# Top-k attention and expert layer on one core: weight pieces through a queue, and the first three batches routed sooner

## The chip, the core and the metric

The kernel runs on one core of a Trainium2 chip. A core has TensorE (PE: matmuls, with the weight loads PEld beside them), VectorE (DVE), ScalarE (ACT), GpSimd (POOL) and SyncE (SP, which here issues most DMAs). They run side by side and wait for each other by semaphores. The metric is the device time of one execution in microseconds (us), as the median of several runs; lower is better.

## What is computed

Attention over 8 batches of 8 heads, 576 rows of 64 numbers, where each row of scores keeps its 32 largest; then an expert layer, in which each of the 4608 rows of 512 numbers goes to the one of 8 experts that its logits choose:

```python
scores = scale * np.matmul(q, k.transpose(0, 1, 3, 2))
kth = np.partition(scores, -top_k, axis=-1)[..., -top_k:-top_k + 1]
scores = np.where(scores >= kth, scores, -1000000000.0)
attn = np.exp(scores - np.max(scores, axis=-1, keepdims=True))
attn = attn / (np.sum(attn, axis=-1, keepdims=True) + 1e-09)
x = np.matmul(attn, v)          # then (B, H, S, D) -> (B * S, H * D)

logits = x @ w_gate + modality_bias[modality_id]
e_idx = np.argmax(logits, axis=1)
gate_w = probs[np.arange(N), e_idx]      # probs: softmax of the logits
for e in range(E):
    mask = e_idx == e
    h = np.maximum(x[mask] @ w1[e], 0.0)
    out[mask] = gate_w[mask, None] * (h @ w2[e])
```

## The kernel before

The attention is cut into 288 tiles of 128 rows by 576 scores; nine tiles make the two heads of a pair, four pairs a batch, so a batch is 36 steps. One loop (`for i in range(LAST)`, L1105) runs over all tiles, one per step, as a pipeline: step `i` makes the scores of tile `i + 2` on PE (`scores`, L1113), lets ACT copy them to `Ssb` (`sevac`, L385), and on DVE takes the largest of six pieces of tile `i` (`subs`, L391) and merges those of tile `i - 1` (`chain`, L396). The sign of the scores against the 24th largest (ACT, `sign`, L421) times the scores (POOL, `pool_y`, L429, tile `y`) gives DVE the next eight (`find`, L434). The 32nd is then known, and the exponentials below it are dropped. For two in three of the first 48 tiles this goes by `hide` on DVE, `hidden` on POOL (tile `ex`, L469) and `masked` on ACT; for all others by `expo` on ACT and `keep` on DVE (tile `P`, L456), and POOL reads one element of `P` as a gate (L479). Nine steps later PE transposes the probabilities (`trans`), ACT copies them, and PE multiplies them by v (`av`, L518). `j = i % 9` is the place in a pair.

For the pairs ahead, q and k are loaded on SP's queue at `j` 5 and 6, v at 7; PE transposes them (`prep`) at `j` 0 (the tail), 1 (k) and 3 (q), and DMAs on the same SP queue stack their halves one step later (`moves`: tiles `ks` at L332, `qs` at L334). The scores need both.

Once a batch is through, it is routed in steps counted by `r`: logits (L563) at r 0, their transposes (L572) and DVE's products `lt` (L580) at r 1, the rows of x (L551, L552) at r 2 to 4, then `route`: a one-hot `ohb` of the best expert, ACT's exponential `r_ez`, rank matmuls against triangular matrices (`ranks`, L597) and ACT's copy `r_rk`, the sum `r_sm`, and the places `dest`. Five indirect DMAs of POOL (`send`, L609) scatter the rows into a buffer `xs` sorted by expert. The small DVE steps stand in the list `side`, of which each step takes up to 12, to the next `PAUSE`; `rush` goes ahead of it.

As soon as rows enough are there (`more_moe`, L873), a slot of 256 rows of one expert is picked, gathered (`rows`, L699, tile `xg`) and computed in small pieces, which each step takes as long as a budget in microseconds, `spare_pe`, allows: transposes of the rows, `hid` (w1, L790) and `outp` (w2, L802). The weights of a slot are eight DMAs of 512 KB on SP's queue, four pieces of `w1b` (L722) and four of `w2b` (L726); each goes out when the slot before has used its piece (`used`, L736), or from the lists of `more_moe`. Slots 0 to 13 are computed beside the attention, slots 14 to 18 after it at higher precision (`slot`, L1043). Where PE has no expert work, `keep_warm` (L950) gives it matmuls of constants whose results nobody reads.

Of the kernel before, what the change touches and what calls it, by code (L numbers as in the profile page):

```python
# [13 lines left out]
AF = mybir.ActivationFunctionType  # L14
# [15 lines left out]
NW = 3  # L30
# [14 lines left out]
TL = LR + 2  # L45
# [12 lines left out]
PJ0 = (1, 2, 3)  # L58
FAST = 7
RXQ = (2, 3, 3, 4, 4)  # L60
SNQ, RNQ = 12, 18
# [14 lines left out]
def kernel(  # L76
# [13 lines left out]
    V, A, G, PE, SP = nc.vector, nc.scalar, nc.gpsimd, nc.tensor, nc.sync  # L90
    B, H, S, D = q.shape
# [493 lines left out]

    def route(lg, bias, oh, x5b, wait=0):

# [19 lines left out]
        def send(c):  # L607
# [14 lines left out]
                                    op=OP.is_equal),  # L622
            PAUSE,
            *[PAUSE] * wait,
            lambda: A.activation(ez, z, AF.Exp),
            ranks,
            PAUSE,
# [27 lines left out]
    def sched(s, whole):  # L655

        o = {"w1": {}}
        SL[s] = o  # L660
# [63 lines left out]

    def load_w2(s, g):
        SP.dma_start(w2b[:, 2 * g:2 * g + 2, :],  # L726
                     w2[ds(SL[s]["e"], 1), g * 256:g * 256 + 256, :].rearrange("o (c p) d -> p (o c) d", p=128))

    def expert(s, act, nxt, whole, defer):
# [6 lines left out]
        def used(x, load):  # L736

            o["used"][x] += 1
            if o["nxt"]:
                chore.append(lambda g=o["used"][x] - 1: load(s + 1, g))  # L740
                if not defer:
                    chores()
# [31 lines left out]
        def xt_next(c):  # L774
# [7 lines left out]
            SL[s + 1]["early"] = c == 2  # L782

        def hid(f, c0):
            if f % 2 == 0 and c0 == 0:
                room()
                o["ps"] = tile_e([128, 2, SLOT], f // 2)
            ps = o["ps"]
            for c in range(c0, c0 + HG):
                PE.matmul(ps[:, f % 2], w1b[:, c, f * 128:(f + 1) * 128], xgT[:, c, :],  # L790
                          start=(c == 0), stop=(c == KC - 1))
            if f % 2 == 0 or c0 + HG < KC:
                return
            post(lambda: A.activation(hT[:, f - 1:f + 1, :], ps, AF.Relu) if act else  # L794
                 V.tensor_scalar(hT[:, f - 1:f + 1, :], ps, 0.0, None, op0=OP.max))
            used(0, load_w1)

        def outp(f, t):
            if f == 0:
                room()  # L800
                o["py"] = tile_e([128, Dm], t)
            PE.matmul(o["py"], hT[:, f, t * 128:(t + 1) * 128], w2b[:, f, :], start=(f == 0), stop=(f == FC - 1))  # L802
            if f % 2 == 1 and t == 1:
                used(1, load_w2)
            if f == FC - 1:
                post(lambda py=o["py"]: result(t, py))
# [63 lines left out]
    plan = {"ready": -1, "go": False}  # L870
    alone = [False]

    def more_moe():  # L873
# [14 lines left out]
        elif full >= n + 1:  # L888
# [11 lines left out]
            def take(x, g):  # L900
                return lambda: (load_w1, load_w2)[x](n, g) if g < free[x] else None
            l1 = [take(0, g) for g in range(4)]
            l2 = [f for g in range(4) for f in (take(1, g), PAUSE)]
            go = [lambda: plan.update(go=True)]
            if n == 0:
                def sent():

                    while sends:
                        sends.popleft()()
                rush.extend(pick + [begin] + l1[:2] + done + [PAUSE, sent] + rows + go + [PAUSE, l1[2], l1[3], PAUSE] + tok)  # L910
            else:
                begun, rest = ([], go) if moe else (go, [])
                rush.extend(pick + [begin] + rows + rest + l1[:1] + done + [PAUSE, l1[1], l1[2], PAUSE, l1[3]] + begun + [PAUSE] + tok)
# [71 lines left out]
    for x in range(QL):  # L985
# [5 lines left out]
        sevac(x)  # L991
    keep_warm(NW)
    ok = lambda x: 0 <= x < NT
# [111 lines left out]
    for i in range(LAST):  # L1105
# [48 lines left out]
        cost += COST["rest"] * (len(lp) > 0)  # L1154
        part = (PREP if p else PREP0).get(j)
        if p + 1 < NPAIR and part:
            prep(p + 1, part)
            cost += COST["t" if part == "t" else "prep"]
        if p + 2 < NPAIR and j in LJ:
            load(p + 2, "kq"[LJ.index(j)])  # L1160
        if j == VJ and p < NPAIR:
            load(p, "v")
        b1, r = divmod(i - (TL + 2), 36)
        b1 -= 1
        if 0 <= b1 < B:
            if r == 0:
# [13 lines left out]
            if r == rl[1] + (1 if early_route(b1) else 2):  # L1180
                steps, store = route(lgb[b1 % 2], bias_all[:, b1], ohb[b1 % 2], x5, int(FAST <= b1 < B - 1))
                side.extend(steps)

                def done(n=b1 + 1):
                    seen[0] = n * S
                    fresh.clear()
                if b1 == 0:
                    side.extend([store.pop(), done])
            if r == max(rl[1], rx[4]) + (1 if early_route(b1) else 2):
                if b1 == 0:  # L1190
# [10 lines left out]
        if ok(u) and role(u) in (3, 7, 8):  # L1201
            f = av(u // 9, role(u), xTs(u // 36)[(u // 9) % HP])
            if role(u) == 7:
                avs.extend(f)
            else:
                f[0][1]()
                avs.extend(f[1:])
                cost += f[0][0]
# [63 lines left out]
        arrange(ops, *end)  # L1272

        for f in moves:
            f()
# [19 lines left out]
        if ok(i - 2) and (i - 2) % 3 == 2:  # L1295
            small(i - 4)
        if i == CLOSE:
            alone[0] = True
            S0 = nslot[0]
# [159 lines left out]
```

## Time and profile before

| | us |
|---|---|
| median of 3 runs | 1208.47 (1208.12 to 1208.58) |
| the profiled execution | 1207.26 |
| its span, first to last instruction | 1205.5 |
| PE busy in the span | 1158.7 |
| DVE busy | 1100.4 |
| ACT busy | 982.4 |
| POOL busy | 677.0 |

The profile is one execution, whose every instruction has a start and a duration. A view by line groups equal instructions; the timeline shows them in order with the idle time ahead of one and what ended it; the waits sum this idle time; the busy time by stretch shows when an engine was full, and the granted clock of TensorE as a share of 2.4 GHz (1.00, or 0.50 for 1.2 GHz). An engine's idle time costs only where others wait for it.

### The profile page before, as it was taken

Reading aid. Unit: us, or ns where it says so; the run is one execution under the profiler, and the core shown is the slowest. Engines: PE = TensorE matmul, PEld = TensorE weight load, DVE = VectorE, ACT = ScalarE, POOL = GpSimd, SP = SyncE. Lnnn points to the kernel's source line nnn. Section 1 sums busy time; section 2 is a strip of 40 time slices with the busy share of each in tenths; the row PEclk is TensorE's granted clock in tenths of the full one; section 3 lists DMA queues with packets and bytes.
Section 4 is the critical chain, followed back from the end, with each engine's and each line's share of the span. In section 5 each row is a group of like instructions: output and inputs, shape, how many; then the busy total and the mean of one; then the engine's idle time right before and its main releaser. Section 6 shows DMA issues by size and latency. Waiting matters only on the chain.

```text
span 1205.5 us, 28005 instructions
## 1 busy us (share of the span) xinstructions
PE 1158.7 (96%) x7914; PEld 908.5 (75%) x7914; DVE 1100.4 (91%) x5474; ACT 982.4 (81%) x2015; POOL 677.0 (56%) x1256
## 2 busy tenths in 40 slices
PE   8889979999999999999899999999999999999998
PEld 6766767778687877778587776878687777589987
DVE  7999999999999999999999999999998999376772
ACT  6999979998798988998799888989898888355652
POOL 6888875564755566556556566557655655121011
PEclk9899999999999999999999999999999999999999
DMA  5563358663585638664865657665665653287750
GB/s 127 157 180 88 88 157 228 170 166 88 158 235 146 166 103 256 159 168 122 215 184 145 173 148 192 171 158 148 169 194 146 177 156 123 82 274 248 254 196 22
DMA packets 204323, 197.09 MB, mean 163 GB/s; under 512 B 104413, under 2 KB 151533, under 8 KB 204160
## 3 DMA queue, kind: packets, MB, share of 16 engines
q1 hardware_dynamic: 196880, 175.92, 53.6%
q0 software_dynamic: 6080, 19.00, 4.3%
q8 instruction: 66, 1.08, 0.4%
q14 instruction: 97, 0.79, 0.2%
q10 hardware_dynamic: 1200, 0.30, 0.1%
HBM read 118.63 MB, written 24.23 MB: 119 GB/s over the span
## 4 chain that ended last, share of the span: by engine, by line
PE 47%; DVE 38%; ACT 5%; DMA 5%; issue 3%; SPq 1%; POOL 1%; POOLq 0%; ACTq 0%; DVEq 0%
DVE cand L394 10%; PE E L802 8%; PE E L790 7%; PE X L518 7%; DVE P L456 6%; DVE mg L436 6%; PE S L382 5%; PE T L490 5%; PE X L1067 5%; PE X L1051 4%; DVE cand L405 2%; DVE cand L406 2%; DVE x L552 2%; DVE mg L407 2%; PE E L1051 1%
## 5 line engine op out<-in xcount | busy, mean ns | idle before, releaser
L394 DVE MAX8 cand<-Ssb 128x8 f32<-128x96 f32 x1728 | 387.5, 244 | 1.8 <-ACT Ssb L387 1.8
L432 POOL TENSOR_TENSOR y<-Ssb,K 128x576 f32<-128x576 f32 x288 | 368.0, 1278 | 36.1 <-ACT K L426 35.0
L382 PE MATMUL S<-ks,qs 128*128 128x288 f32 x992 | 222.3, 346 | 19.7 <-ACT Ssb L387 10.2
L387 ACT ACTIVATE Ssb<-S 128x576 f32<-128x576 f32 x284 | 187.7, 661 | 58.5 <-PE S L382 33.0
L426 ACT ACTIVATE K<-Ssb,n 128x576 bf16<-128x576 f32 x288 | 230.1, 799 | 5.7 <-POOL y L432 5.0
L436 DVE MAX8 mg<-y 128x8 f32<-128x576 f32 x288 | 213.2, 740 | 4.7 <-POOL y L432 4.7
L382 PEld LDWEIGHTS S<-ks,qs 128*128 128x128 f32 x992 | 153.4, 192 | 68.4 <-issue 26.6
L790 PE MATMUL E<-xgT,w1b 128*128 128x256 f32 x832 | 201.1, 384 | 2.2 <-ACT hT L794 1.1
L450 ACT ACTIVATE ex<-Ssb,sm 128x576 f32<-128x576 f32 x256 | 202.6, 791 | 0.0
L456 DVE SCALAR_TENSOR_TENSOR P<-Ssb,kth,ex 128x576 f32<-128x576 f32 x230 | 193.4, 841 | 8.1 <-ACT ex L450 7.0
L498 ACT ACTIVATE PT<-T 128x640 f32<-128x640 f32 (+1 forms) x288 | 193.6, 672 | 7.6 <-PE T L490 7.5
L802 PE MATMUL E<-w2b,hT 128*128 128x512 f32 x416 | 195.9, 599 | 0.5 <-ACT hT L794 0.2
L490 PE MATMUL T<-idf,P 128*128 128x128 f32 x1152 | 170.1, 275 | 6.5 <-ACT P L475 5.8
L790 PEld LDWEIGHTS E<-xgT,w1b 128*128 128x128 f32 x832 | 151.2, 190 | 29.2 <-ACT hT L794 7.1
L479 POOL TENSOR_SCALAR spare<-P 1x1 f32<-1x1 f32 x230 | 41.5, 181 | 194.3 <-DVE mg L405 165.4
L490 PEld LDWEIGHTS T<-idf,P 128*128 128x128 f32 x1152 | 137.8, 141 | 13.2 <-ACT P L475 10.0
L518 PE MATMUL X<-PT,vm 128*64 128x256 f32 (+1 forms) x1536 | 145.5, 332 | 1.2 <-DVE x L552 1.2
L518 PEld LDWEIGHTS X<-PT,vm 128*64 128x64 f32 x1536 | 88.5, 138 | 45.3 <-issue 10.7
L419 POOL TENSOR_SCALAR n<-mg 128x1 f32<-128x1 f32 x288 | 71.7, 249 | 90.3 <-DVE mg L407 67.5
L802 PEld LDWEIGHTS E<-w2b,hT 128*128 128x128 f32 x416 | 73.8, 192 | 61.2 <-issue 57.4
L1073 POOL DMA_INDIRECT out_dram<-ot,tk x12 | 12.2, 1020 | 94.5 <-ACT ot L1072 94.5
L426 ACT ACTIVATION_READ_ACCUMULATOR K<-Ssb,n 128x1 f32 x288 | 64.0, 222 | 0.0
(223 smaller groups left out, 2159.2 us busy)
## 6 DMA issues: line engine op xcount, KB each, us to landing
w1b<-in_moe_w_dram SPq DMA_DIRECT2D x76, 512.0 KB, 5.2
w2b<-in_moe_w_dram SPq DMA_DIRECT2D x76, 512.0 KB, 4.5
ks<-st SPq DMA_DIRECT2D x62, 288.0 KB, 4.2
ks<-st SPq DMA_DIRECT2D x62, 256.0 KB, 4.9
qs<-st SPq DMA_DIRECT2D x124, 128.0 KB, 4.4
xg<-xs SPq DMA_DIRECT2D x19, 516.0 KB, 4.3
vm<-in_v_dram SPq DMA_DIRECT2D x32, 256.0 KB, 4.3
km<-in_k_dram SPq DMA_DIRECT2D x63, 128.0 KB, 3.7
```

The lines of the kernel that those rows point to most:

```text
L382: PE.matmul(ps[:, hf, :288], l, m, start=(n == 0), stop=(n == len(terms) - 1))
L394: return [lambda s=s: V.max(c[:, s * 8:s * 8 + 8], T[i]["S"][:, bnd[s]:bnd[s + 1]]) for s in range(NSUB)]
L426: A.activation(t["K"], t["S"], AF.Sign, scale=2.0 ** -24 - 1.0, bias=t["n"][:, 1, i % 3:i % 3 + 1], accum_out=t["n"][:, 0, i % 3:i % 3 + 1])
L432: G.tensor_tensor(t["y"], t["S"], t["K"], op=OP.mult)
L436: V.max(t["mg"][:, i % 3, 24:32], t["y"])
L450: A.activation(t["ex"], t["S"], AF.Exp, bias=t["s"][:, i % 3:i % 3 + 1])
L456: V.scalar_tensor_tensor(t["P"], t["S"], kth[:, i:i + 1], t["ex"], op0=OP.is_ge, op1=OP.mult, accum_out=dn)
L490: PE.transpose(T[i]["pt"][:, x, :], (Pm if c == 4 else Pb[c % 2])[:, h * 512 + x * 128:h * 512 + x * 128 + 128], idf)
L498: A.activation(o, T[i]["pt"][:, :n], AF.Copy)
L518: PE.matmul(o.rearrange("p (a b) -> p a b", a=2) if j < 8 else o, l, r, start=(c == 0), stop=(c == 4))
L790: PE.matmul(ps[:, f % 2], w1b[:, c, f * 128:(f + 1) * 128], xgT[:, c, :], start=(c == 0), stop=(c == KC - 1))
L802: PE.matmul(o["py"], hT[:, f, t * 128:(t + 1) * 128], w2b[:, f, :], start=(f == 0), stop=(f == FC - 1))
```

## The change

Weight pieces no longer go to SP when they are asked for. They enter a list `wl`, of which each step sends one, before the stacking DMAs, and none at `j` 3 and 4 (q is prepared at 3 and stacked at 4). Before a matmul that reads a piece, the list is emptied as far as that piece (`loaded`), so that the program's order stays right; from step `CLOSE` on pieces go out at once. The first three batches (`SOON`) are routed one step sooner: their last `av` of the 36 tiles runs in its own step and not in the next, the k part of `prep` in the step of their logits moves one step back, the one-hot, the ranks and the exponential stand in one step (ranks first), and the rows are scattered from two steps sooner on. The first slot is started (`go`) two pauses after its gather is asked for. After the first two score tiles, one `keep_warm(NW)`, six matmuls, is left out; it is the only work that differs in number.

```diff
 FAST = 7
+HOLD = (3, 4)
+SOON = 3
 RXQ = (2, 3, 3, 4, 4)
...
-    def route(lg, bias, oh, x5b, wait=0):
+    def route(lg, bias, oh, x5b, wait=0, soon=False):
...
                                     op=OP.is_equal),
-            PAUSE,
-            *[PAUSE] * wait,
-            lambda: A.activation(ez, z, AF.Exp),
-            ranks,
+            *[PAUSE] * (wait + 1 - soon),
+            *[lambda: A.activation(ez, z, AF.Exp), ranks][::-1 if soon else 1],
             PAUSE,
...
-        o = {"w1": {}}
+        o = {"w1": {}, "w2": {}}
         SL[s] = o
...
     def load_w2(s, g):
+        SL[s]["w2"][g] = True
         SP.dma_start(w2b[:, 2 * g:2 * g + 2, :],
...
             if o["nxt"]:
-                chore.append(lambda g=o["used"][x] - 1: load(s + 1, g))
+                chore.append(lambda g=o["used"][x] - 1: weight(lambda: load(s + 1, g)) if defer else load(s + 1, g))
                 if not defer:
...
+        def loaded(what, g):
+            while defer and g not in o[what]:
+                wl.popleft()()
+
         def hid(f, c0):
+            loaded("w1", f // 2)
             if f % 2 == 0 and c0 == 0:
...
         def outp(f, t):
+            loaded("w2", f // 2)
             if f == 0:
...
     alone = [False]
+    wl = deque()
+
+    def weight(f):
+
+        if alone[0]:
+            f()
+        else:
+            wl.append(f)
...
             def take(x, g):
-                return lambda: (load_w1, load_w2)[x](n, g) if g < free[x] else None
+                return lambda: weight(lambda: (load_w1, load_w2)[x](n, g)) if g < free[x] else None
             l1 = [take(0, g) for g in range(4)]
...
                         sends.popleft()()
-                rush.extend(pick + [begin] + l1[:2] + done + [PAUSE, sent] + rows + go + [PAUSE, l1[2], l1[3], PAUSE] + tok)
+                rush.extend(pick + [begin] + l1[:2] + done + [PAUSE, sent] + rows + [PAUSE, PAUSE] + go + [l1[2], l1[3], PAUSE] + tok)
             else:
...
         sevac(x)
-    keep_warm(NW)
     ok = lambda x: 0 <= x < NT
...
         part = (PREP if p else PREP0).get(j)
+        if 1 <= p // HP <= SOON and p % HP == 1 and j in (1, 2):
+            part = PREP.get(1) if j == 2 else None
         if p + 1 < NPAIR and part:
...
             load(p, "v")
-        b1, r = divmod(i - (TL + 2), 36)
+        b1, r = divmod(i - (TL + 1), 36)
+        if b1 > SOON:
+            b1, r = divmod(i - (TL + 2), 36)
         b1 -= 1
+        soon = b1 < SOON
         if 0 <= b1 < B:
...
             if r == rl[1] + (1 if early_route(b1) else 2):
-                steps, store = route(lgb[b1 % 2], bias_all[:, b1], ohb[b1 % 2], x5, int(FAST <= b1 < B - 1))
+                steps, store = route(lgb[b1 % 2], bias_all[:, b1], ohb[b1 % 2], x5, int(FAST <= b1 < B - 1), soon)
                 side.extend(steps)
...
                     side.extend([store.pop(), done])
-            if r == max(rl[1], rx[4]) + (1 if early_route(b1) else 2):
+            if r == (rx[2] + 1 if soon else max(rl[1], rx[4]) + (1 if early_route(b1) else 2)):
                 if b1 == 0:
...
             f = av(u // 9, role(u), xTs(u // 36)[(u // 9) % HP])
-            if role(u) == 7:
+            if role(u) == 7 and not (u % 36 == 35 and u // 36 < SOON):
                 avs.extend(f)
...
+        if wl and j not in HOLD:
+            wl.popleft()()
         for f in moves:
...
         if i == CLOSE:
+            while wl:
+                wl.popleft()()
             alone[0] = True
```

POOL at the first batch's scatters. `ex` and `y` are a step's two large products; `xs<-x,dest` is a scatter. Before:

```order
L469 TENSOR_TENSOR ex<-Ssb,hT 128x576
L432 TENSOR_TENSOR y<-Ssb,K 128x576
L609 DMA xs<-x_155,dest 38912x516
L535 MEMSET spare 1x1
L609 DMA xs<-x_155,dest 38912x516
L535 MEMSET spare 1x1
L419 TENSOR_SCALAR n<-mg 128x1
L469 TENSOR_TENSOR ex<-Ssb,hT 128x576
L609 DMA xs<-x_155,dest 38912x516
L535 MEMSET spare 1x1
L432 TENSOR_TENSOR y<-Ssb,K 128x576
```

After:

```order
L471 TENSOR_TENSOR ex<-Ssb,hT 128x576
L434 TENSOR_TENSOR y<-Ssb,K 128x576
L611 DMA xs<-x_155,dest 38912x516
L537 MEMSET spare 1x1
L611 DMA xs<-x_155,dest 38912x516
L537 MEMSET spare 1x1
L421 TENSOR_SCALAR n<-mg 128x1
L611 DMA xs<-x_155,dest 38912x516
L537 MEMSET spare 1x1
L481 TENSOR_SCALAR spare<-P_120 1x1
L434 TENSOR_TENSOR y<-Ssb,K 128x576
```

The scatters stand two steps sooner against the tiles. Between the third scatter and the `y` after the last, one `ex` is gone: the tile of that step is one of those that take the gate instead.

SP where the seventh slot's weights are asked for, in the fifth batch of tiles: `ks` and `qs` are the stacking of k and q, and one piece of `w1b` stands right ahead of these rows in both orders. Before:

```order
L332 DMA ks<-st 64x2x576 x2
L332 DMA ks<-st 64x2x512
L332 DMA ks<-st 64x2x64
L332 DMA ks<-st 64x2x512
L332 DMA ks<-st 64x2x64
L722 ISA
L722 DMA w1b<-in_moe_w_dram 128x4x256
L722 ISA
L722 DMA w1b<-in_moe_w_dram 128x4x256
L722 ISA
L722 DMA w1b<-in_moe_w_dram 128x4x256
L334 DMA qs<-st 64x512 x4
```

After:

```order
L334 DMA ks<-st 64x2x576 x2
L334 DMA ks<-st 64x2x512
L334 DMA ks<-st 64x2x64
L334 DMA ks<-st 64x2x512
L334 DMA ks<-st 64x2x64
L336 DMA qs<-st 64x512 x4
L144 DMA km<-in_k_dram 128x4x64 x2
L145 DMA kqt<-in_k_dram 64x2x64
L722 ISA
L722 DMA w1b<-in_moe_w_dram 128x4x256
```

The three pieces of `w1b` that stood between the stacking of k and that of q now follow it one by one, behind the loads of the next pair.

PE at the second batch's logits (L563, then L565) and their transposes (L572, then L574). Before:

```order
L518 MATMUL X<-PT,vt_81 64x64 x2
L382 MATMUL S<-ks,qs 128x288 x4
L490 MATMUL T<-idf,P_119 128x128 x5
L295 MATMUL X<-st,nid 128x512
L563 MATMUL X<-xT,wgt 32x512 x4
L563 MATMUL X<-xT,wgt 32x64 x4
L382 MATMUL S<-ks,qs 128x288 x4
L490 MATMUL T<-idf,P_120 128x128 x4
L316 MATMUL X<-idf,qm 128x128 x4
L572 MATMUL X<-idf,x_155 128x128 x4
L572 MATMUL X<-idf,x_155 64x128
```

After:

```order
L492 MATMUL T<-idf,P_119 128x128 x4
L297 MATMUL X<-st,nid 128x128
L565 MATMUL X<-xT,wgt 32x512 x4
L565 MATMUL X<-xT,wgt 32x64 x4
L520 MATMUL X<-PT,vm 64x64 x8
L520 MATMUL X<-PT,vt_81 64x64 x2
L384 MATMUL S<-ks,qs 128x288 x4
L492 MATMUL T<-idf,P_119 128x128 x5
L318 MATMUL X<-idf,km 128x128 x4
L574 MATMUL X<-idf,x_155 128x128 x4
L574 MATMUL X<-idf,x_155 64x128
```

The large `av` (64x256) has moved out ahead of these rows, the logits come before the small one, and the transposes of k, not of q, stand ahead of the logit transposes.

## Rows read from the trace of the kernel before

**Rows 1.** The page, busy us (share) xinstructions of each engine

```profile
PE 1158.7 (96%) x7914; PEld 908.5 (75%) x7914; DVE 1100.4 (91%) x5474; ACT 982.4 (81%) x2015; POOL 677.0 (56%) x1256
```

**Rows 2.** Busy time by stretch: us; PE, PEld, DVE, ACT, POOL busy; PEclk, DMA, GB/s

```profile
190.00:1012.00 822.00, 807.13 (x5396) 620.34 (x5395) 802.70 (x4243) 724.42 (x1500) 491.99 (x952) 1.00 0.61 167
1012.00:1206.00 194.00, 185.94 (x1181) 157.64 (x1179) 118.44 (x268) 97.27 (x157) 34.97 (x70) 0.99 0.52 175
```

**Rows 3.** DVE's waits, 30 to 1012 us: total us, times, longest

```profile
DVE lt L580 <- PE X L572: 12.0, 6, 2.1
DVE P L456 <- ACT ex L450: 5.3, 10, 1.7
DVE mg L436 <- POOL y L432: 3.7, 1, 3.7
```

**Rows 4.** Timeline of the start: start us, us, engine, line, operation [idle before]

```profile
10.37 1.70 PE L954 MATMUL E<-onesb 128*128 128x256 bf16 x12
10.89 0.65 ACT L387 ACTIVATE Ssb<-T 128x576 f32<-128x576 f32 x1
12.00 0.41 PE L367 MATMUL S<-ks 64*128 64x288 f32 x1
...
18.04 0.76 DVE L436 MAX8 mg<-y 128x8 f32<-128x576 f32 x1 [0.24 <-POOL y L432]
...
21.23 0.76 DVE L436 MAX8 mg<-y 128x8 f32<-128x576 f32 x1 [0.76 <-POOL y L432]
```

**Rows 5.** Busy time by stretch, around three clock readings

```profile
10.00:24.00 14.00, 13.81 (x129) 11.16 (x127) 12.00 (x82) 10.24 (x23) 6.58 (x14) 1.00 0.45 116
...
28.40:38.60 10.20, 8.93 (x54) 7.23 (x53) 10.20 (x53) 7.88 (x20) 8.57 (x12) 0.50 0.34 84
...
595.00:598.40 3.40, 2.97 (x10) 2.51 (x11) 3.40 (x21) 1.22 (x2) 1.30 (x3) 0.50 0.66 166
```

**Rows 6.** Timeline of the first batch's scatters, POOL and DVE

```profile
173.94 1.27 POOL L469 TENSOR_TENSOR ex<-Ssb,hT 128x576 f32<-128x576 f32 x1 [1.15 <-DVE hT L463]
...
176.60 1.05 POOL L609 DMA_INDIRECT xs<-x,dest  x1 [0.16 <-issue]
...
179.92 1.27 POOL L469 TENSOR_TENSOR ex<-Ssb,hT 128x576 f32<-128x576 f32 x1
181.35 0.94 POOL L609 DMA_INDIRECT xs<-x,dest  x1 [0.15 <-issue]
...
182.35 1.27 POOL L432 TENSOR_TENSOR y<-Ssb,K 128x576 f32<-128x576 f32 x1
...
183.66 0.76 DVE L436 MAX8 mg<-y 128x8 f32<-128x576 f32 x1 [3.74 <-POOL y L432]
```

**Rows 7.** Timeline of the second batch's routing, DVE and ACT

```profile
285.17 0.39 DVE L580 TENSOR_TENSOR lt<-X,rd 128x128 f32<-128x128 f32 x1 [2.08 <-PE X L572]
...
294.65 0.67 DVE L552 TENSOR_TENSOR x<-X,rd 128x512 f32<-128x512 f32 x1
...
295.25 0.21 ACT L605 ACTIVATE r_rk<-X 128x48 f32<-128x48 f32 x1 [2.58 <-PE X L604]
...
295.52 0.17 DVE L628 TENSOR_REDUCE r_sm<-r_ez 128x5 f32<-128x40 f32 x1
```

**Rows 8.** Timeline around the seventh slot's weights, SP's queue, PE and DVE

```profile
583.13 3.15 SPq L722 DMA_DIRECT2D w1b<-in_moe_w_dram  x3
...
595.43 1.30 PE L382 MATMUL S<-ks,qs 128*128 128x288 f32 x4 [3.93 <-DMA qs<-st]
...
605.54 0.82 DVE L456 SCALAR_TENSOR_TENSOR P<-Ssb,kth,ex 128x576 f32<-128x576 f32 x1 [1.67 <-ACT ex L450]
```

**Rows 9.** The chain of waits, two stackings of q: start us, us, what

```profile
24.69 2.35 DMA qs<-st
...
588.12 7.18 DMA qs<-st
```

**Rows 10.** The page, DMA issues: xcount, KB each, us to landing

```profile
w1b<-in_moe_w_dram SPq DMA_DIRECT2D x76, 512.0 KB, 5.2
```

## The prediction

> **What bounds the kernel now.** I read the busy shares first, then the busy time by stretch, then VectorE's (DVE's) waits inside the main loop, then the places where those waits lie. The shares name no winner: TensorE (PE) 1158.7 us and DVE 1100.4 us of 1205.5 [rows 1]. By stretch the two part. Between 190 and 1012 us DVE is busy 802.70 of 822.00 us and PE 807.13; after 1012 us PE is busy 185.94 of 194 us and DVE 118.44 [rows 2]. So the loop over the score tiles is paced by DVE with PE hardly behind it, and the tail (the last expert slots) by PE. PE's busy time is modelled; DVE's waits are the firmer reading. From 30 to 1012 us DVE waits 21.0 us in three groups worth a line: 12.0 us for the logit transposes, 5.3 us for ACT's exponentials, 3.7 us for one y of POOL [rows 3]. Since no DVE instruction is added or taken away, the change can only win in the loop what lies in those waits and in the two short ones of the start, and can only lose by making new ones. The tail does not change: the build order has the same expert pieces left in both kernels from the end of the loop on, and slots 14 to 18 follow in both.
>
> **The start: six warming matmuls less.** Twelve warming matmuls stand together and take 1.70 us, six of them 0.85 [rows 4]. Behind them come the score matmuls of 12.00, which need a PSUM bank that ACT empties until 10.89 + 0.65 = 11.54. So they can come 0.46 us earlier and no more. DVE waits 0.24 and 0.76 us at 18.04 and 21.23 for y, which hangs on ACT and so on these scores [rows 4]; both can take up a shift of 0.46. I take -0.45, with 0 and -0.85 as ends. What could eat it: PE stands idle until 11.54. The clock was granted in full from 10 to 24 us and at half (1.2 GHz) from 28.4 to 38.6, behind a gap in PE's work [rows 5]. The Trainium skill (TensorE: Matmul & The Clock Gate, What's actually happening) lets the array fall to half rate when PE has been idle, which is what warming matmuls are there against. By that rule the stretch of 10 to 24 us could cost several us instead of winning 0.45; the trace shows full clock there with gaps of 0.3 us before such matmuls, so I keep the row's answer.
>
> **The first batch: routing and scatter two steps sooner.** The 3.74 us wait at 183.66 is POOL's [rows 6]. From 173.94 POOL does without a pause ex, y, scatter, scatter, a small one, ex, scatter, y and ends at 182.35 + 1.27 = 183.62: 9.68 us. DVE in that time does two plain steps and has no more to do from 183.66 - 3.74 = 179.92 on: 5.98 us. The difference, 3.70, is the wait. The change shifts the five scatters two steps to the front. POOL's list from the same point is then ex, y, scatter, scatter, small, scatter, gate, y: one ex less, since the third of every three tiles has none. That is 9.68 - (181.35 - 179.92) + 0.2 = 8.45 us. DVE's two steps now hold two of the x rows, at 0.67 each [rows 7]: 5.98 + 1.34 = 7.32. The wait left is 1.1 us, the gain 2.6. The ends: 3.74 if DVE's step has more in it, 0 if the wait only moves with the scatters. DVE's small steps of routing are the same ones, packed in three steps where there were four; POOL, ACT and PE wait longer there, and nobody waits for them, for scores run two steps ahead of DVE. The slot itself begins in the same step as before, now three steps behind its gather.
>
> A scatter takes 1.05 us beside a busy DVE and 0.94 while DVE waits [rows 6]: five of them beside a busy DVE could cost POOL 0.11 each, 0.55 us more. The Trainium skill (SBUF — State Buffer, SBUF: two separate sides) says that the descriptors of a DMA issued by POOL cannot be written while DVE runs an instruction that takes the port which both share. By that rule alone the scatters, moved beside DVE's densest steps, would stretch until the wait of 3.74 is back, and the sum would be 2.6 us poorer. The two rows show a tenth of a microsecond of it, and what the rule would make of the time is the second rival.
>
> **Second and third batch: logits a step sooner.** In both, DVE waits for the logit transposes, 2.08 us at 285.17 in the second [rows 7]; PE is behind there with its own work. The change moves the last average-value matmuls a step up, holds the k transposes back by one, and takes one pause out, so one-hot, rank matmuls and exponential stand in one step. Up to the transposes PE's list holds the same things in one step less, with one expert piece fewer ahead of them in the second batch; DVE comes to them one step sooner too. I take no change for these waits. New is the order behind it. Today ACT's copy of the ranks ends at 295.25 + 0.21 = 295.46 and the first DVE step behind the pause starts at 295.52 [rows 7], needing only the exponential, which had been done for 2.6 us. Afterwards the exponential comes behind the ranks, and PE must first wait for a one-hot of the same step. The margin of today, 0.06 us on ranks that are not yet needed, would be used up; I take +0.3 us for both batches together, with ends of -1.0 (half of one wait of 2.08 gone) and +2.5 (what ACT waits there today, 2.58, seen once by DVE).
>
> **The queue of weight pieces.** No bytes change: 512 KB pieces, at most one a step and none in the two steps around q's stacking. What it can win is seen once: at 595.43 PE waits 3.93 us for q's stacked scores operand [rows 8]. Three pieces stand in SP's queue directly ahead of it (583.13), and the stacking takes 7.18 us to land; the one of the program's start, with no piece ahead, took 2.35 [rows 9]. After the wait PE runs 3.4 us at half clock [rows 5], and DVE loses 1.67 us at 605.54 for an exponential that came late through PE [rows 8]. In the new order one piece and k's stacking are all that stands ahead. PE's wait should fall below 1 us, the clock stay up, and DVE's 1.67 go: -1.7, ends -0.8 and -2.8 (with the smaller waits for exponentials of the same batch, out of 5.3 us in ten [rows 3]). What the queue delays is the weights; by the build order each piece is issued at least four steps before its first matmul, some 12 us, and a piece lands in 5.2 us by the median [rows 10]. So no price there. From the third batch on, expert pieces stand some four places earlier against the loop, and the later waits for logit transposes move with them: -0.5, ends -1.5 and +0.5.
>
> **The sum.** -0.45 - 2.6 + 0.3 - 1.7 - 0.5 = -4.95 us. The profiled execution took 1207.26 us, 1.76 of it around its span, and lies 1.21 below the median of 1208.47. I set the difference against the median: 1208.47 - 4.95 = 1203.5.
>
> **The rivals.** 1. PE paces the loop, not DVE: every wait of PE that goes comes back in full. For it speaks PE's 807 of 822 us; against it that DVE's waits are the same 2.1 us with and without a long wait of PE before them. PE would gain 3.93 + 1.7 of half clock, once more about 2.5 + 1.7 where the third slot's gather is waited for, and DVE's share would be at most what it waits: some 4 us more than forecast, 1199.5. 2. The scatter wait moves with the scatters, because they lengthen beside a busy DVE: the 2.6 fall away, 1206.1. For it speaks 1.05 beside 0.94, against it that the difference is small. 3. The queue does not do what it says: q's stacking waits in SP for its own operand, and lands no sooner. Then 1.7 and most of the 0.5 fall away, 1205.6; for it speaks that SP spends time on the k stacking's own waits there, against it 7.18 beside 2.35. 4. Slower: the rank matmuls wait on PE for the one-hot of their own step, in the two loaded batches. PE loses there what ACT loses today at the ranks, 2.58 us [rows 7], and a clock step of 1.7 behind it, and DVE stands at the exponential's sum for both: 4.3 us a batch, 8.6 in two, against 5.25 won elsewhere: +3.4, 1211.8. It decides from the point where PE reaches the ranks before the one-hot is done and DVE then reaches the sum before ACT has copied. Against it: PE is behind DVE at that place today, so it should find the one-hot ready.
>
> **How the numbers follow.** Forecast 0.57, PE-paced 0.08, scatter wait moves 0.13, queue without effect 0.13, slower 0.09. The ends of the terms, not all at once, give 1200 to 1207 for the forecast itself; taking in the second and third rival, and one bad turn in the second batch, the range is 1199.5 to 1208.5. A measurement of this kernel can tell about 0.2% from no change, 2.4 us: faster is below 1206.1. The forecast case lies there nearly whole (0.55), the first rival too, the third for three quarters and the second for half: 0.78 in all; slower 0.08, the same 0.14.
>
> **What would show it.** Right: DVE's wait for y behind the first scatters is 0 to 2 us; no wait of PE for q's stacking over 1 us around the seventh slot's weights, and clock 1.00 there; DVE's waits for exponentials sum to about 3 us instead of 5.3; the waits for the logit transposes stay near 12. Wrong: a DVE wait at the exponential's sum in the second or third batch, a PE wait for a weight piece, or a half-clock stretch in the first 25 us.

## The result and the profile after

| | before | after |
|---|---|---|
| median of 6 runs each, us | 1208.68 (1208.12 to 1212.50) | 1194.09 (1193.43 to 1197.07) |
| ratio | | 0.9877, 95% interval 0.9859 to 0.9896 |
| the profiled execution, us | 1207.26 | 1193.59 |
| its span, us | 1205.5 | 1191.9 |

The change wins 14.6 us, where 5.0 were forecast, and ends below the range. The busy shares after, against [rows 1]:

```profile
PE 1153.1 (97%) x7908; PEld 904.7 (76%) x7908; DVE 1093.2 (92%) x5474; ACT 983.2 (82%) x2015; POOL 675.8 (57%) x1256
```

DVE runs the same 5474 instructions and is busy 7.2 us less. So much could not come out of its waits: between 25 us and the loop's end these fell from 21.0 us [rows 3] to 15.8, as DVE's waits after show (total us, times, longest):

```profile
DVE lt L582 <- PE X L574: 12.7, 6, 2.6
DVE P L458 <- ACT ex L452: 1.7, 4, 0.5
DVE mg L438 <- POOL y L434: 1.2, 1, 1.2
DVE P L458 <- issue: 0.2, 1, 0.2
```

Half of the gain in the loop lies inside instructions that the page counts as busy. The next table says where. It is worked out from the traces: the time between DVE's first `cand` of one tile and that of a later one (tile t stands in step t), before, and the difference to it in three other profiles. These are single executions, and the differences of their spans lie up to 1.1 us from those of the medians.

| stretch | before, us | after | queue alone | routing alone |
|---|---|---|---|---|
| to tile 48 | 152.1 | -0.8 | -0.7 | +1.2 |
| 48 to 60, first batch routed | 50.6 | -2.7 | +0.1 | -2.7 |
| 60 to 168 | 383.1 | -0.7 | -0.1 | +1.2 |
| 168 to 192, behind the seventh slot's weights | 83.2 | -5.1 | -5.3 | -2.4 |
| 192 to 204 | 48.7 | +0.1 | 0.0 | +0.1 |
| 204 to 228 | 80.2 | -2.2 | -1.2 | -0.2 |
| 228 to the last score matmul | 207.4 | -0.3 | -0.5 | +1.9 |
| from there to the end | 200.3 | -2.0 | 0.0 | -2.0 |
| the span | 1205.5 | -13.6 | -7.6 | -2.9 |

### The profile page after: what moved, and what is told of

Its sections match the earlier page's. It is cut to its first block, busy times and chain, and to the rows that moved or that the text cites. A ratio compares the mean times of both kernels' runs of the same rounds, so it can differ in the third digit from the quotient of the medians.

```text
span 1191.9 us, 28040 instructions
## 1 busy us (share of the span) xinstructions
PE 1153.1 (97%) x7908; PEld 904.7 (76%) x7908; DVE 1093.2 (92%) x5474; ACT 983.2 (82%) x2015; POOL 675.8 (57%) x1256
## 4 chain that ended last, share of the span: by engine, by line
PE 61%; DVE 27%; ACT 6%; issue 2%; POOL 2%; DMA 1%; SPq 1%; POOLq 0%; ACTq 0%; DVEq 0%
PE E L809 12%; PE E L796 10%; PE X L520 9%; PE S L384 7%; DVE cand L396 7%; PE T L492 6%; PE X L1081 5%; DVE mg L438 4%; PE X L1065 4%; DVE P L458 4%; PE E L1065 1%; DVE cand L407 1%; ACT K L428 1%; DVE cand L408 1%; ACT Ssb L389 1%
```

## What the stretch from 168 to 192 shows

The largest piece is the place of [rows 8]. Busy time by stretch, from tile 168 to tile 192, first before, then after (us; PE, PEld, DVE, ACT, POOL busy; granted clock, DMA share, GB/s):

```profile
585.76:668.95 83.19, 78.72 (x492) 58.91 (x492) 80.54 (x420) 70.26 (x145) 48.97 (x93) 0.98 0.66 184
```

```profile
581.58:659.68 78.10, 78.01 (x501) 59.77 (x501) 77.96 (x421) 70.51 (x145) 47.79 (x95) 1.00 0.71 205
```

Before, PE is idle for 4.47 us and loses about 1.5 us to the half clock of [rows 5] (it is busy for 2.97 us there, from 595.43 to 598.40); what is left, 77.2 us, is its work. After, the stretch is 78.1 us long and PE is busy throughout; its one loss is a wait of 0.66 us for a gather just ahead (575.38). PE loses 5.3 us less, and 5.1 us have come back, while DVE's idle time there gives back only 2.5 (2.65 to 0.14). The other 2.6 us are DVE's busy time, 80.54 to 77.96, for the same instructions.

Where they sat is seen when DVE's and POOL's rows are laid side by side. The timeline before, at two places behind the late scores (start us, us, engine, line, operation):

```profile
608.01 1.33 DVE L683 TENSOR_SCALAR s_oh<-s_key,s_m,s_sc 128x8 f32<-128x8 f32 x1
608.03 1.29 POOL L432 TENSOR_TENSOR y<-Ssb,K 128x576 f32<-128x576 f32 x1 [1.31 <-ACT K L426]
...
642.12 1.37 POOL L432 TENSOR_TENSOR y<-Ssb,K 128x576 f32<-128x576 f32 x1 [1.25 <-ACT K L426]
642.54 0.99 DVE L444 TENSOR_TENSOR jk<-eq,mg 128x27 f32<-128x27 f32 x1
```

and the timeline after, in a step that runs as it should:

```profile
613.80 1.27 POOL L434 TENSOR_TENSOR y<-Ssb,K 128x576 f32<-128x576 f32 x1
615.14 0.17 DVE L445 TENSOR_TENSOR eq<-i9s,n 128x27 f32<-128x27 f32 x1
```

`jk`, 27 numbers a partition, lasts 0.99 us and ends at 643.53, when y ends (643.49); `s_oh`, 8 numbers, lasts 1.33 us, as long as its y. `eq` alone takes 0.17. The order is laid out so that `eq` comes just behind y (615.14 behind 615.07). When y is late, because ACT's K is late, because the scores are late, the small DVE instruction meets a running y and is held to its end, and the profile calls that busy. No wait of DVE tells of it. Over the stretch, `eq`, `jk` and `s_oh` together take 6.0 us before and 3.2 after.

The second reading is the **lead**: how long before DVE's first `cand` of a tile ACT has finished its copy. At tile 174 the copy (605.40 + 0.65) is 1.2 us ahead of DVE before, and 6.4 us after (594.70 + 0.68):

```profile
605.40 0.65 ACT L387 ACTIVATE Ssb<-S 128x576 f32<-128x576 f32 x1
607.24 0.25 DVE L394 MAX8 cand<-Ssb 128x8 f32<-128x96 f32 x1
```

```profile
594.70 0.68 ACT L389 ACTIVATE Ssb<-S 128x576 f32<-128x576 f32 x1
601.77 0.25 DVE L396 MAX8 cand<-Ssb 128x8 f32<-128x96 f32 x1
```

Over before and after together, from tile 60 on and outside the routing steps, three steps in which the lead stays above 3.5 us take 9.5 us in the median, and most such groups no more than 9.6; where it falls below 2.5 us they take 9.7 to 9.8 in the median, and single groups over 12. (Which tiles are put into a group moves these numbers a little.) DVE waits for the logits once a batch, and the lead is refilled there to 6 to 8 us and used up over the rest of the batch. What PE loses early in a batch is missing until the next refill.

## The experiments

Three theories were held against each other: the forecast's (DVE paces, PE's delays cost what DVE visibly waits), the lead theory (PE's losses come back in full, late and in drawn-out DVE instructions), and, inside it, the hold theory (small DVE instructions are held by a running y).

### The parts alone

**Queue alone.** `before` with the hunks of `wl`, `weight`, `loaded` and this one:

```diff
+        if wl and j not in HOLD:
+            wl.popleft()()
         for f in moves:
```

> The kernel before with the weight queue alone (list wl, one piece a step, none at j 3 and 4). Forecast's theory (DVE paces, PE's delays cost only what DVE visibly waits): -1.7 to -2.2 us, 1206.3 to 1206.8. Rival theory (lead: every microsecond that PE loses eats the lead that the scores have over DVE, and below some 3 us of lead it comes back in full, also as DVE instructions that are drawn out): PE's wait of 3.93 us, the half clock behind it and the slow steps up to the end of the next batch come back, -5 to -8 us, 1200.5 to 1203.5. The wait for the third slot's gather near 322 us should stay under both.

Measured 1200.01, ratio 0.9925 (0.9897 to 0.9952), -8.7 us: somewhat more than the lead theory asked, four times the forecast's. From 168 to 192 it wins all that the whole change wins, and the wait for the third slot's gather stays (2.30 us at 321.60).

**Routing alone.** `before` with all hunks of `SOON` and the two pauses, weights sent at once:

```diff
-        b1, r = divmod(i - (TL + 2), 36)
+        b1, r = divmod(i - (TL + 1), 36)
+        if b1 > SOON:
+            b1, r = divmod(i - (TL + 2), 36)
```

> The kernel before with the earlier routing of the first three batches alone, the two pauses ahead of the first slot's start among it; weights go out at once as before. Forecast's theory: -2.3 us (2.6 of the first batch, less 0.3), 1206.2. Lead theory: besides the first batch's 2.5 us, PE's wait of 3.33 us for the third slot's gather and the half clock behind it go, -6 to -8 us, 1200.5 to 1202.5; PE's wait of some 4 us for q's stacking near 590 us should stay under both.

Measured 1206.02, ratio 0.9975 (0.9954 to 0.9996), -2.7 us. That is the forecast's number by luck: by the table the first batch gives the 2.7 us, and -2.4 and -2.0 elsewhere cancel against +1.2, +1.2 and +1.9. The lead theory's number failed: the gather's wait is gone, but its gain doesn't show. Two things took it. PE used the time for expert work that now stands earlier (348 `hid` matmuls by tile 156 instead of 332), and only 2.0 us come back at the end, where eight `outp` matmuls fewer are left. And the shifted weight pieces now stand ahead of other stackings of q. PE's waits for DMAs between 200 and 1000 us, routing alone:

```profile
PE S L383 <- DMA qs<-st: 5.8, 4, 2.0
PE S L383 <- DMA kqt<-in_k_dram: 2.1, 1, 2.1
PE X L779 <- DMA xg<-xs: 1.1, 1, 1.1
```

The parts fall short of the whole (-8.7 and -2.7 against -14.6). The medians alone could not tell 3.2 us, given their intervals, but the rows show where some of it lies: the earlier routing makes new waits for q, and with the queue PE's only wait for a DMA in that stretch of time is one of 0.7 us for a gather.

**Warming matmuls alone.**

```diff
         sevac(x)
-    keep_warm(NW)
```

> The kernel before without the six warming matmuls behind the first two score tiles, nothing else changed. Forecast's theory: -0.45 us, 1208.0, with the DVE waits of 0.24 and 0.76 us near 18 and 21 us shorter. Rival: the two half-clock stretches of the start change in length and with them the time: -0.8 us where the first of them ends earlier, up to +3 us where the clock falls in the first 25 us.

Measured 1209.22, ratio 1.0005 (0.9988 to 1.0023): nothing that the time can tell. In the trace the first six tiles take 12.93 us instead of 13.35, and 12.93 or 12.94 in all profiles without these matmuls (13.34 to 13.36 in the three with them). That is -0.41 against a forecast of -0.45. Two things cover it: DVE's first step starts between 8.6 and 9.8 us from execution to execution, and the half-clock stretches at 28 and 175 us differ in length (3.4 to 10.3 us). They also make the +1.2 of routing alone in the first line of the table: 0.6 is a later first step, 0.6 lies in tiles 6 to 36.

### PE's time and DVE's holds, each by itself

**28 more matmuls on PE, at three places.** In the changed kernel:

```diff
+        if i == 171:
+            keep_warm(14)
```

> The changed kernel with 28 more warming matmuls (whose results nobody reads, some 4.0 us of PE work) in step 171, where the scores lead DVE by 4 to 6 us and nothing waits for PE. Forecast's theory (DVE paces): 0 to +1 us over the changed kernel, 1194 to 1195. Lead theory: the lead is gone, later steps are drawn out until the next long step gives it back: +3 to +4.5 us, 1197 to 1198.5, in DVE waits for exponentials and in small DVE instructions that last as long as POOL's y.

Measured 1198.64, ratio 0.9915 (0.9885 to 0.9945), against 1194.58 for the changed kernel measured again (below). The 28 matmuls take 3.2 us, not the 4.0 that were expected:

```profile
592.56 3.22 PE L969 MATMUL E<-onesb 128*128 128x256 bf16 x28
```

From tile 168 to 192:

```profile
581.12:664.37 83.25, 83.11 (x535) 63.56 (x535) 81.20 (x421) 71.21 (x146) 48.86 (x95) 1.00 0.69 194
```

83.25 us against 78.10 and 79.27 in the changed kernel's two profiles. Not all of the difference is the edit's: just ahead of the stretch PE waits 2.44 us for a gather here, and 0.66 and 1.86 us there, and this wait costs its length (shown below). With it taken off, 80.81 stand against 77.44 and 77.41: 3.2 us of work cost 3.4, though nothing waits for them where they stand. DVE's visible waits are 1.9 us of the stretch; its busy time for the same 421 instructions grew by 3.2 over the first profile, 2.9 of it in `eq` and `jk`. This is the length of before (83.19), made again out of PE's time alone.

The same in step 201, where the lead is 8 us (`if i == 201:`):

> The changed kernel with the same 28 warming matmuls (some 4.0 us of PE work) in step 201 instead of 171, just behind the long routing steps, where the scores lead DVE by 8 us. Rival (only a sudden shortage counts, a lead of 8 us swallows 4): 0 to +1 us over the changed kernel, and the steps behind 201 as long as before. Lead theory: the lead falls by 4 us for the whole batch of tiles, the loss comes late, in steps 210 to 228 where the lead was 2 to 3 us: +3.5 to +5.5 us, 1197.5 to 1199.5.

Measured 1197.05, ratio 0.9895 (0.9826 to 0.9964). Tiles 192 to 204 take 48.81 us as before the edit (48.85), tiles 204 to 228 take 80.89 instead of 77.97. The loss comes late, as the lead theory has it, and is 2.9 us for 3.2 us of work. A lead of 8 us doesn't swallow it. (These are two runs; their median is half a microsecond below the range, which had counted 4 us of work.)

The same in step 36, where PE has no expert work (`if i == 36:`):

> The changed kernel with the same 28 warming matmuls (some 4.0 us of PE work) in step 36, where no expert work runs and PE stands idle for a tenth of the time. Lead theory: the lead falls from 4.4 us to near zero, is refilled within some ten steps out of PE's idle time, and no later step knows of it: 0 to +1.5 us over the changed kernel, 1194 to 1195.5. If each microsecond of PE work cost its time wherever it stands: +4 us, 1198.

Measured 1196.79, ratio 0.9903 (0.9871 to 0.9935). Tiles 36 to 48 take 39.65 us instead of 37.83, +1.8 for 3.2 us of work, a little over what was allowed; a held `jk` (1.0) and a wait of 0.5 us for logit transposes are most of it. The lead falls to 1.7 us at tile 40 and is back at 5.1 by tile 48, and no later stretch of the loop moves by more than 0.4: here PE's idle time refills the lead. In this profile 0.9 us more lie ahead of the edit, and 0.8 behind the loop.

**y made late, PE left alone.** Four tiny POOL instructions ahead of y in every third step from 168 to 239:

```diff
+        if 168 <= i < 240 and (i - LT) % 3 == 2:
+            for _ in range(4):
+                G.tensor_scalar(spare[:, 0:1], spare[:, 0:1], 1.0, 1.0, op0=OP.mult, op1=OP.mult)
         if ok(i - LY):
             pool_y(i - LY)
```

> The changed kernel with four tiny POOL instructions (1x1, some 0.18 us each) ahead of y in every third step from 168 to 239, 24 times; y then starts some 0.7 us later, and its reader on DVE comes 1.8 us behind the end of y, so no semaphore makes DVE wait. Forecast's theory (only DVE's waits cost): 0 to +1 us. Hold theory (a small two-operand DVE instruction that starts beside a running y lasts until y ends): eq, or the instruction behind it, is drawn out by some 0.4 to 0.7 us each time, +8 to +15 us, with no more idle time of DVE.

Measured 1209.03, ratio 1.0009 (0.9992 to 1.0027), +14.5 us over the changed kernel. Groups by line from tile 168 to 240, the changed kernel, then with the late y (xcount | busy us, mean ns of one | idle before):

```profile
L445 DVE TENSOR_TENSOR eq<-i9s,n 128x27 f32<-128x27 f32 x24 | 7.1, 297 | 0.0
```

```profile
L445 DVE TENSOR_TENSOR eq<-i9s,n 128x27 f32<-128x27 f32 x24 | 22.8, 951 | 0.0
```

and the busy time of that kernel from tile 168 to 192:

```profile
581.29:665.53 84.24, 84.15 (x561) 64.11 (x560) 84.10 (x420) 75.09 (x155) 53.85 (x127) 1.00 0.69 194
```

One instruction went from 297 to 951 ns, 24 times: 15.7 us, as much as the whole loss. DVE's idle time did not grow: from tile 168 to 240 it waits 5.3 us for y in four steps, where the changed kernel waits 4.9 us for transposes and exponentials. From 168 to 192 DVE is busy 84.10 of 84.24 us: by busy time it was never fuller, and it did nothing more. The Trainium skill (SBUF — State Buffer, Who interferes with whom) says that a VectorE instruction with two SBUF inputs and a GpSimd instruction that reads SBUF exclude each other, and that the later one is blocked until the first ends. The trace agrees: 22 of the 24 `eq` end within 0.05 us behind y, as the held `eq` and `jk` of the other traces do.

### The rest of the queue, and three versions that were to be better

**Without the two empty steps.**

```diff
-HOLD = (3, 4)
+HOLD = ()
```

> The changed kernel with the queue but without its two empty steps (HOLD empty): one weight piece a step also where q is prepared and stacked. If one piece a step is what matters: within 1 us of the changed kernel, 1193 to 1195. If the empty steps matter: one piece of 512 KB stands ahead of q's stacking in several pairs, PE waits some 2 us for it in each of these, and the lead theory makes of it +2 to +5 us, 1196 to 1199.

Measured 1198.58, ratio 0.9918 (0.9879 to 0.9957), +4 us. PE waits for q's stacking again, at three later places (between 200 and 1000 us):

```profile
PE S L384 <- DMA qs<-st: 3.6, 3, 1.7
PE X L311 <- DMA kqt<-in_q_dram: 0.9, 1, 0.9
PE X L781 <- DMA xg<-xs: 0.8, 1, 0.8
```

The five runs lie between 1195.74 and 1203.81, so the size is rough; in the trace 1.9 us are lost in tiles 204 to 228 and 1.8 from tile 240 to the last scores, where these waits lie. One piece a step alone is not enough.

**Earlier routing for seven batches.**

```diff
-SOON = 3
+SOON = 7
```

> The changed kernel with the earlier routing for the first seven batches instead of three. Lead theory: the gathers of later slots (PE waits 0.7 to 1.5 us for one near 575 us) come earlier and expert work can start sooner, which puts a little more of it beside the loop: -1 to -3 us, 1191 to 1193. Forecast's theory, by its term for the second and third batch (+0.3): +0.6 us, 1194.7.

Measured 1204.91, ratio 0.9968 (0.9944 to 0.9992), +10 us, which neither theory foresaw. DVE's waits for the logit transposes grow from 12.7 to 15.1 us (the longest 3.5 instead of 2.6), the loop is 4.0 us later by tile 282, and the other six come behind it: 2.8 up to the last scores and 3.2 from there to the end. The cause of these six was not followed up; behind the loop PE waits 1.38 and 1.05 us near 1055 us and then runs 3.4 us at half clock, none of which the changed kernel has.

**Scatters one a step.** In the long routing steps two scatters a step stand behind y on POOL, and the next y is late by them. One a step from the second batch on, and the gather two steps later:

```diff
-                                [PAUSE] * 3 * (b1 < FAST) + [store[-1], done])
+                                [PAUSE] * 5 * (b1 < FAST) + [store[-1], done])
...
-            for _ in range(min(1 + quick, len(posted))):
-                posted.popleft()()
+            posted.popleft()()
```

> The changed kernel with one scatter of routed rows a step instead of two from the second batch on, and five pauses instead of three ahead of the next gather, so that no gather runs ahead of its scatters. Hold theory: with two scatters of 1.0 to 1.3 us behind y the next y starts up to 0.9 us late, and in each batch a P and an eq are drawn out by 0.57 and 0.92 us; with one scatter these go, about 1.5 us in each of six batches: -4 to -9 us, 1185 to 1190. Rival (the later gather costs more: expert work starts two steps later in each batch and the lead is lost elsewhere): 0 to +4 us, 1194 to 1198.

Measured 1216.87, ratio 1.0074 (1.0045 to 1.0103), +22.3 us. The holds went as foreseen (tiles 192 to 204 take 47.3 us instead of 48.8, and so in three batches), and the later gather cost far more than the rival asked. PE's waits for DMAs between 200 and 1000 us:

```profile
PE E L796 <- DMA w1b<-in_moe_w_dram: 4.2, 1, 4.2
PE X L781 <- DMA xg<-xs: 4.1, 2, 3.1
PE E L809 <- DMA w2b<-in_moe_w_dram: 2.9, 1, 2.9
```

They lie between 319 and 463 us, and tiles 84 to 120 take 13.7 us more. Again this is PE's loss in full: 10.1 us of these waits fall there (3.08, 4.16 and 2.90), and PE runs at half clock for 3.4 us behind each of the last two, which costs 3.4 us together: 13.5 in all.

**Scatters spread in the fourth to seventh batch alone**, begun one step earlier:

```diff
-            if r == (rx[2] + 1 if soon else max(rl[1], rx[4]) + (1 if early_route(b1) else 2)):
+            if r == (rx[2] + 1 if b1 < FAST else max(rl[1], rx[4]) + (1 if early_route(b1) else 2)):
...
-            for _ in range(min(1 + quick, len(posted))):
+            for _ in range(min(1 + (quick and soon), len(posted))):
```

(with four pauses for these batches instead of three)

> The changed kernel with the scatters of the fourth to the seventh batch spread: one a step instead of two, begun one step earlier, so that the gather behind them stands in the same step as in the changed kernel. Hold theory: the long routing steps of these four batches are 1.5 us shorter each, as they were where all batches had one scatter a step (192 to 204: 48.8 to 47.3 us). If DVE pays for it and nothing else does: -6 us, 1188. Lead theory with PE as the engine that sets the pace of the loaded loop: PE gets no less work, so the lead that the routing steps build up is smaller by these 1.5 us and the steps behind give back part of it: -1 to -4 us, 1190 to 1193.

Measured 1202.84, ratio 0.9948 (0.9931 to 0.9964), +8.3. Tiles 168 to 192, 192 to 204 and 204 to 228, with the spread scatters:

```profile
580.69:668.80 88.11, 87.32 (x539) 65.78 (x541) 84.00 (x420) 74.72 (x153) 50.40 (x98) 0.97 0.66 186
668.80:716.59 47.79, 46.97 (x351) 37.22 (x347) 45.03 (x239) 41.11 (x87) 29.54 (x55) 1.00 0.48 124
716.59:795.73 79.14, 78.56 (x501) 59.16 (x503) 78.77 (x420) 71.66 (x147) 48.55 (x96) 1.00 0.70 197
```

and in the changed kernel, profiled a second time:

```profile
581.73:661.00 79.27, 79.19 (x505) 60.47 (x506) 79.13 (x420) 70.51 (x146) 47.54 (x95) 1.00 0.72 202
661.00:709.83 48.83, 48.47 (x360) 38.51 (x357) 46.07 (x240) 42.74 (x90) 29.67 (x59) 1.00 0.49 128
709.83:787.79 77.96, 77.38 (x492) 57.82 (x492) 77.75 (x421) 69.95 (x145) 47.44 (x93) 1.00 0.70 196
```

The first line holds an accident. The gather of one slot came later, against the expectation, and PE waited for it:

```profile
580.92 1.11 PE L781 MATMUL X<-idf,xg 128*128 128x128 f32 x4 [5.59 <-DMA xg<-xs]
```

Behind it PE runs 5.9 us at half clock (2.9 us of work). Against the second profile, whose wait there was 1.9 us, PE loses 6.7 us more, and the stretch is 8.8 us longer; the other 2 us were not followed up. The second and third lines are what the version was for: DVE wins 1.04 us in the routing steps and the steps behind give back 1.18. A gain of DVE alone brings nothing there.

**The changed kernel again.**

> The changed kernel itself, unchanged, as the measure for the other runs on this chip: 1194 us, ratio 0.988 to the kernel before; its steps as long as in the first profile within 0.1 us a stretch of 24 steps, but for the length of the two half-clock stretches at 28 and 175 us, which differ from run to run.

Measured 1194.58, ratio 0.9880 (0.9863 to 0.9896). The stretch from 168 to 192 differs by 1.2 us from the first profile (79.27 to 78.10), more than the 0.1 expected; the others of the loop agree within 0.2. The traces show why. PE's wait for the gather just ahead of the stretch, first profile, then second:

```profile
575.38 0.66 PE L781 MATMUL X<-idf,xg 128*128 128x128 f32 x4 [0.66 <-DMA xg<-xs]
```

```profile
576.74 0.65 PE L781 MATMUL X<-idf,xg 128*128 128x128 f32 x4 [1.86 <-DMA xg<-xs]
```

The wait is 1.20 us longer and the stretch 1.17, while DVE is idle for 0.14 us of it in both. The kernels with the extra work in steps 36 and 201 differ from this one only outside the stretch; there the wait is 0.62 and 0.38 us and the stretch 78.03 and 77.82. In all four the stretch less the wait is 77.41 to 77.44: what PE waits costs its full length, and DVE's waits show nothing of it. No version beat the changed kernel.

## Why the prediction was wrong in size

**The step that failed** is the first: that DVE paces the loop, so that "the change can only win in the loop what lies in those waits". From the second batch on both engines are full, and a loss on either costs nearly its full length: of PE (3.2 us of work cost 3.4 in step 171 and 2.9 in step 201; a longer wait for a gather cost its length) and of DVE (the held `eq`). The 5.1 us of the stretch from 168 to 192 are PE's, where the forecast counted the 1.67 that DVE was seen to wait. DVE's 802.70 busy us of 822 [rows 2] were read as work; part of them were holds. The argument brought against the first rival, that DVE waits the same 2.1 us for the transposes with and without a long PE wait ahead [rows 3], is true and proves nothing: that wait refills the lead, the loss lies in the steps ahead of it. The first rival had the mechanism and too small a price: its own list of PE's losses, 3.93 + 1.7 + 2.5 + 1.7 = 9.8 us in place of the 2.2 forecast for these places, would have given 1195.9, but it was held down to what DVE waits, 1199.5.

By the terms of the sum:

- **Start**, -0.45: -0.41 up to tile 6, right, and too small for a measurement. The granted clock stayed at 1.00 from 10 to 24 us; the several microseconds that the Trainium skill's rule (TensorE: Matmul & The Clock Gate, What's actually happening) would have taken there did not come.
- **First batch**, -2.6: -2.72, with the queue and without it. The wait left was put at 1.1 us and is 1.19; the balance of POOL against DVE [rows 6] was the right reading:

```profile
167.89 1.02 POOL L611 DMA_INDIRECT xs<-x,dest  x1 [0.16 <-issue]
169.21 1.00 POOL L611 DMA_INDIRECT xs<-x,dest  x1 [0.20 <-issue]
170.85 0.94 POOL L611 DMA_INDIRECT xs<-x,dest  x1 [0.28 <-issue]
...
173.71 0.76 DVE L438 MAX8 mg<-y 128x8 f32<-128x576 f32 x1 [1.19 <-POOL y L434]
```

  The five scatters take 0.94 to 1.13 us, as long as before the change (0.94 to 1.12), so the second rival is out. What stood beside it from the Trainium skill (SBUF — State Buffer, SBUF: two separate sides), that descriptors of POOL's DMAs can't be written beside certain DVE instructions, shows in none of these rows; where the contention of these two engines is seen to cost time, DVE's small instructions wait for POOL. It isn't absent in the later batches, though: in the second and third, one scatter of the five lasts 1.94 and 1.92 us in the changed kernel, where none of these batches took more than 1.28 before, and a P starts on DVE 0.3 us into it. What that costs was not measured.
- **Second and third batch**, +0.3 with ends of -1.0 and +2.5: -0.7 from tile 60 to 168 with the queue, +1.2 without it (the wait for the third slot's gather, gone here, is in both sums). No wait at the exponential's sum; the fourth rival is out for three batches (with seven the routing does cost time).
- **Queue**, -1.7: -5.1 where it was looked for. The mechanism was right (in the changed kernel PE has no wait for q's stacking there, the clock is 1.00, and no weight piece comes late); the size was taken from DVE's wait of 1.67 us instead of PE's 3.93 and its half clock, some 1.5.
- **Expert pieces earlier**, -0.5: -2.2 from 204 to 228, of which the queue alone has 1.2 (before, PE waits there 1.40 us for ACT at 726.26, with the queue 0.5). What the rest is was not followed up.
- **The tail**, 0: -2.0. The same pieces were left at the end of the loop's last steps, but the loop is paced only as long as scores come. At the last score matmul 32 `outp` matmuls are left instead of 40. The count was right and taken a few steps too late.

The signs listed came as said (DVE's wait behind the scatters, no wait for q, exponentials 1.7 us against some 3, transposes 12.7 against some 12), and none of the signs against it. They could not tell the forecast from the first rival; the length of steps without a wait would have.

## What to carry to other kernels

Where two engines are both over 97% busy, price a loss on the one by that engine's own time, not by what the other is seen to wait: look whether equal steps have equal lengths, and how far the producer is ahead, before calling one of them the pace. A busy share is not work: compare the duration of the same small instruction in quiet and in late steps. And a queue shared by urgent small transfers and patient large ones wants the large ones held back around the urgent ones; one a step was not enough here.

## What the runs showed of the hardware

A DVE instruction with two SBUF inputs of 27 numbers a partition, 0.17 us by itself, lasted up to 1.37 us beside a POOL product of 128x576 (`jk` before), and the held ones ended within 0.05 us of the product's end; MAX8 runs on beside it (0.24 us, as without it). The profile counts the hold as busy. And the half-clock stretch at 28 us lasted 3.4 us in five and 6.8 in five executions of kernels that are the same up to there, and 10.2 in two of others; tiles 6 to 36 took 91.6 to 91.7 us with either of the shorter ones, and 92.2 and 92.8 with 10.2.
